# A block of Fourier filter and MLP on one core: constant tables loaded earlier, a merged first layer, and a new order of the work

## The chip, the cores and the metric

The kernel runs on one core of a Trainium2 chip. The metric is the device time of one execution in microseconds (us). Before the change three runs took 150.68, 151.34 and 151.72 us (median 151.34).

## What is computed

```
xn = layernorm(x)                                     # x: 2048 x 640, bf16
A  = irfft2( rfft2(xn) * (w_r + i*w_i) )              # over both axes
B  = gelu(xn @ w1 + b1) @ w2 + b2                     # 640 -> 1536 -> 640
out = x + A + B
```

## The kernel before

The 2048 rows are sixteen tiles of 128 rows ("tile c"). Two lines of work share the engines.

*The MLP.* DVE takes each tile's statistics (`stats`, line 479, two instructions a tile) and normalises it (`xn_c`, line 509). The result is turned into `xnT`, columns on the partitions: for tiles 0 to 5 by TensorE (`tps`, line 527) and a copy out of PSUM, for tiles 6 to 15 by a transposing DMA from SP's queue (line 518). The first layer multiplies with `W1`, which is loaded in five row blocks (`w1_0` to `w1_4`). For tiles 0 and 1 it runs in six pairs of hidden columns (`hpsa_0` to `hpsa_5`, line 573): a "pair" below is two matmuls of 128 columns, for one row block and one tile, so there are ten for each `hpsa`. For tiles 2-3, 4-7, 8-11 and 12-15 the blocks are `hps0`, `hps1`, `hps2`, `hps3`, each with twelve columns of hidden units (line 595); each is issued in two parts, row blocks 0 to 2 and then 3 and 4. ACT takes the gelu into `gT` (lines 583 and 601). The second layer sums gT with `W2`, which comes in thirds (`w2_0` to `w2_2`), in steps of four matmuls (line 751). For eight tiles (KEEP) it is done early: `kps` steps, and DVE adds the bias and keeps the sum (line 761). For the others it runs at the end (`fps`).

*The filter.* DVE folds the normalised tiles (`xe`, `xf`, lines 539 and 543), TensorE multiplies with table G (`aps`, line 549), ACT or DVE copies the result into `XV` (line 555). Then come, in six groups or four rounds, `bps` (table E, line 625), `cps` (table M, line 643), the product with the weights `W` on DVE (lines 668 and 672), and `dps` (table N, line 677), all in PSUM banks 0 to 3, each set copied out before the next may use the banks. The copies of `dps` go into buffers `U0` to `U7`, of which three exist at a time; each is turned back by two transposing DMAs (`v0` to `v15`, line 693: U0 gives v0 and v1, and so on), which wait in SP's queue. A new U may be written only when both transposes of the U that had its buffer have landed. When all v have landed, `eps` (table GE, line 716) and the last matmuls with table H (line 767) give the filter's part, which is added to the MLP's in PSUM (line 770) and stored from POOL's queue, or SP's for the last two tiles. Four DMAs from POOL's queue (`pre0` to `pre3`, line 562) write x to the output beforehand, once all of W is there.

*The order.* Nothing is scheduled at run time. Each operation has a number, and the string `ORDER` (line 253) lists all of them in one sequence; a word such as `589p:4` is operation 589 on TensorE (p; s SP, d DVE, a ACT, g POOL) with PSUM bank or buffer 4. `arrange` (line 145) gives every engine its part of the list as a strict queue, and `sync` (line 161) adds the semaphore waits that the data and the buffers need. The times in the calls of `load`, the rates, priorities and the argument `hard` serve a planner that wrote the list; the emitted program depends on the list alone. All loads of x, W1, W2, W and the tables run through SP's queue in the list's order.

Of the kernel before, what the change touches and what calls it, by code (L numbers as in the profile page):

```python
# [13 lines left out]
D = 640  # L14
F = 1536
# [238 lines left out]
9s 2a 0d 1d 3g 125p:4 11a 10s 4g 7g 8p:3 5g 12s 13s 14s 15s 54d 55d 16s 17s 56d 60d 57a 18s 58a 59d 121d:1 19s 61d 124p:2 20s 122p:1 52p:7 62d 21s 123d 126a 63d 22s 64g 241p:3  # L254
301p:4 53a 253p:0 23s 277p:5 289p:6 242p 265p:1 24s 302p 127d 290p 266p 254p 25s 278p 133d:0 128p:2 130p:7 279p 26s 129d 255p 131a 291p 243p 132d 303p 27s 267p 306p 68d 246p 294p
28s 282p 283p 66d 258p 270p 259p 69d 284p 247p 271p 292p 65d 268p 248p 249p 70d 295p 67d 307p 308p 71d 280p 136d:0 272p 72g 244p 245p 137d 250p 134d 281p 309p 251a 293p 285p 286p
141d:1 260p 252a 269p 256p 144d 296p 288a 273p 297p 135d 142p:7 287a 147d:0 145p:2 143a 298p 261p 146d 262p 274p 257p 300a 310p 148d 304p 328p:7 263a 73d 343p:2 276a 85d 337p:3
299a 329p 150d:1 84d 344p 264a 322p:6 76d 275a 319p:5 81d 345a 320p 323p 82d 330a 338p 86d 138p:0 321a 74d 139p 324a 83d 305p 75d 331p:5 87d 140a 77d 88g 334p:7 149d 332p 78d
316p:6 152d 79d 151d 335p 311a 80g 317p 173d:1 312a 346p:0 171d 347p 339a 340p:4 92d 174s 336a 341p 98d 153p:1 318a 154p 159d:0 342a 587p:6 156d 348a 172s 97d 588p 155a 163d:0
313p:4 101d 160p:0 116d 29s 589p 100d 30s 314p 93d 590p 31s 315a 162d 32s 157p:3 161a 102d 591p 94d 165d:1 99d 33s 333a 90d 592p 158a 89d 34s 325p:4 593d 326p 35s 355p:5 327a 103d  # L260
113d 36s 370p:0 91d 166d 37s 371p 167d 117d 358p:7 95d 164d 38s 96g 108d 356p 176d:0 6g 379p:6 104g 357a 118d 114d 168p:1 175d 372a 169p 184d:0 364p:5 170a 180d:1 185s 179d 365p
177d 359p 197d:1 366a 115d 380p 199d 198s 186d 373p:4 381a 178d 119d 201d:0 376p:5 120g 360a 106d 187s 182p:0 202d 377p 206d:0 181p 109d 378a 374p 200s 204d 105d 367p:6 183a 205d
110d 368p 107d 203d 39s 352p:7 188d:0 369a 40s 189d 207p:0 375a 208p 111d 41s 223d:0 112g 353p 209a 225d 406p:6 42s 190d:1 212d:1 397p:5 43s 192d 354a 191d 407p 193d 44s 210d 398p
215d:0 408a 211s 195p:0 214d 194p 399a 388p:6 219d:1 216d 196a 226s 389p 218d 217d 412p:4 227d:0 228d 221p:1 45s 220p 229d:0 385p:7 222a 213s 231d 230d 413p 232d 386p 390a 46s
234p:0 233p 414a 400p:5 47s 236d 235a 394p:6 48s 387a 457p:0,0 224s 401p 458d 459a 49s 395p 391p:4 396a 460p:0,1 361p:6 461d 462a 362p 409p:7 363a 475p:0 402a 418p:6 476d:0 477a:1
# [31 lines left out]
def bass_parallel_sum__spectral_gfnet__dense_activation_gelu__prompt_kernel(  # L297
# [21 lines left out]
    with ExitStack() as es:  # L319
# [110 lines left out]
        load_x(0, 1, next(pr), at=3.05)  # L430
        load_x(1, 1, next(pr), at=3.5)
        load(part(gT, 0, 1, 0, [[1, F]]), b1v, B_b1t, 3072, q="act", prio=409, at=3.2)
        for j, at in enumerate((5.3, 6.5, 7.7, 9.8, 10.9)):
            if j == 3:
                load_x(2, 2, next(pr), at=8.6)
            load(W1[:, F * j:F * j + F], w1v[:, j, :], B_w1s[j], 393216, prio=next(pr), at=at)
        load(gtab[:], const["G"], B_g, 524288, prio=next(pr), at=12.2)
        for c in range(4, 16, 2):
            load_x(c, 2, next(pr))
        load(b2bc[:], bass.AP(tensor=b2v.tensor, offset=b2v.offset, ap=[[0, 128], [1, D]]), B_b2b, 163840, prio=next(pr))  # L440
        for g in range(3):
            load(W2[:, 4 * g:4 * g + 4, :], w2v[:, g, :, :], B_w2s[g], 4 * D * 256, prio=next(pr))
        load(etab[:], const["E"], B_e, 204800, prio=next(pr))
        load(mtab[:], const["M"], B_m, 65536, rate=200e3, prio=next(pr))
        load(ntab[:], const["N"], B_n, 49152, rate=200e3, prio=next(pr))
        WP = 32 * KP

        def load_w(wsrc, p0, off, row, n, step):
            w_ops.append(load(bass.AP(tensor=Wf, offset=p0 * WP + off, ap=[[2 * WP, 16], [2 * KP, n], [1, 321]]),
                 bass.AP(tensor=wsrc.tensor, offset=wsrc.offset + row * 321, ap=[[128 * 321, 16], [step * 321, n], [1, 321]]),  # L450
                 B_w, 16 * 642 * n, after=[wpad], rate=145e3, issue=0.645, group="W", prio=next(pr)))
# [10 lines left out]
        load(htab[:].rearrange("p a b -> p (a b)"), const["H"], B_h, 524288, prio=next(pr))  # L462
# [103 lines left out]
        for b in range(6):  # L566
            hps = Buf(f"hpsa_{b}", psum, 1, ANY)
            pr = PRIO["hps"] + 2 - b / 10
            head = []
            for t in range(2):  # L570
                part_ = []
                for j in range(5):
                    part_ = [pe([("128", 2 * mm_us(128))], pr - j - t, lambda hps=hps, b=b, t=t, j=j: [
                        (psb(hps.slot, [[1, 128]], 256 * h + 128 * t), view(W1, F * j + 512 * (b // 2) + 2 * (b % 2) + h, [[4, 128]]), xnT[:, t, j, :], t == j == h == 0, j == 4) for h in range(2)],
                        reads=[B_w1s[j], B_xnT[t]], writes=[hps], hard=part_ + head)]
                    head = head or part_
                    l1_ops += part_
                    l1_of.setdefault(t, []).extend(part_)
            for h in range(2):
# [56 lines left out]
        for P in range(4):  # L636
# [53 lines left out]
            for pair, U, B_u in zip(two, Us, B_us):  # L690
                for qq in range(2):
                    q = 2 * pair + qq
                    K.op([("sp", 1.28)], 2000, lambda e, _, q=q, qq=qq, U=U, uv=uv: e.dma_start_transpose(  # L693
                        XV[:, :, 128 * q:128 * q + 128], uv(U, D * qq, [[1, D]])), reads=[U, B_u], writes=[B_v[q]], dma=(163840, 200e3), group=f"v{q // 2}")
# [116 lines left out]
```

## Time and profile before

| | |
|---|---|
| three runs | 150.68, 151.34, 151.72 us |
| the profiled execution's own time | 151.68 us |
| its span, first to last instruction | 149.9 us |
| busy: TensorE, weight loads, DVE, ACT, POOL | 141.9, 90.3, 111.6, 72.5, 21.9 us |
| granted TensorE clock | 1.0 throughout |
| read from and written to HBM | 13.54 MB, 5.24 MB |

The page of the profile names an instruction by engine, line, operation and out<-in; a chain at its end shows which work released which. A matmul's duration includes its run through the array, so the distance from start to start tells what a stream costs. A row of the timeline merges equal neighbours: start, length, engine, what, count, and in brackets the idle time before and what ended it. In the view of windows each engine has its busy time and, in brackets, its instructions. Some matmul records are missing (18 of the 180 first halves of the second layer's 640 columns).

### The profile page before, as it was taken

The numbers are of one execution on the slowest core, as the hardware profiler recorded it, in microseconds if no ns is written. First come the engines' busy times: TensorE is split into PE (matmuls) and PEld (weight loads), VectorE is DVE, ScalarE is ACT, GpSimd is POOL, SyncE is SP. The second block draws the span as 40 slices with busy tenths as digits, with TensorE's granted clock in tenths as the row PEclk, the third lists the DMA queues.
The fourth block names the chain that finished last, engine by engine and source line by source line (L and its number), as shares of the span: only waits on it lengthen the run. The fifth ranks groups of instructions, "written<-read, shape, count | busy, mean of one in ns | idle before, by whom it ended". The sixth has DMA issues, their size and how long they took to land.

```text
span 149.9 us, 4022 instructions
## 1 busy us (share of the span) xinstructions
PE 141.9 (95%) x1708; PEld 90.3 (60%) x1726; DVE 111.6 (74%) x238; ACT 72.5 (48%) x122; POOL 21.9 (15%) x35
## 2 busy tenths in 40 slices
PE   7999998999799999999999997999999999999993
PEld 7899985556366645446545443445676655665662
DVE  2789997999773449959877969720499889999612
ACT  3519995398577669674655734465124020031000
POOL 1101220421100040000000000000002611770420
PEclk9999999999999999999999999999999999999999
DMA  4999998996799939104600530798103392797192
GB/s 114 349 408 396 319 361 176 167 130 137 144 166 178 137 67 406 56 4 86 148 0 4 111 69 4 136 164 163 34 0 41 38 182 93 89 133 89 8 123 90
DMA packets 28499, 20.68 MB, mean 138 GB/s; under 512 B 18881, under 2 KB 25793, under 8 KB 28482
## 3 DMA queue, kind: packets, MB, share of 16 engines
q1 hardware_dynamic: 25888, 15.51, 47.7%
q0 software_dynamic: 2592, 4.92, 17.6%
q8 instruction: 13, 0.21, 0.6%
q14 instruction: 4, 0.03, 0.1%
q10 hardware_dynamic: 2, 0.00, 0.0%
HBM read 13.54 MB, written 5.24 MB: 125 GB/s over the span
## 4 chain that ended last, share of the span: by engine, by line
PE 74%; DMA 12%; SPq 6%; ACT 3%; DVE 2%; issue 2%; DVEq 0%
PE ps L383 73%; DMA W<-in_B_w_dram 9%; SPq L375 5%; DMA XV<-U 3%; ACT XV L394 2%; ACT gT L601 1%; DVE U L395 1%; DVE Xb L395 1%; DVE T L668 0%; SPq L693 0%; DVE Z L672 0%; DVE W L770 0%; PE ps L527 0%; DVEq L233 0%
## 5 line engine op out<-in xcount | busy, mean ns | idle before, releaser
L383 PE MATMUL ps<-xnT,W 128*128 128x512 bf16 (+2 forms) x360 | 58.3, 309 | 1.1 <-ACT XV L394 1.0
L383 PE MATMUL ps<-W,gT 128*128 128x128 bf16 (+3 forms) x378 | 56.6, 291 | 2.4 <-issue 1.4
L383 PEld LDWEIGHTS ps<-W,gT 128*128 128x128 bf16 x396 | 30.0, 98 | 24.2 <-issue 2.2
L383 PEld LDWEIGHTS ps<-xnT,W 128*128 128x128 bf16 x360 | 31.5, 114 | 17.9 <-ACT XV L394 1.5
L601 ACT ACTIVATE gT<-ps,b1col 128x512 bf16<-128x512 f32 (+1 forms) x48 | 28.5, 641 | 12.2 <-PE ps L383 12.0
L777 POOL DMA_DIRECT2D out_dram<-W x14 | 12.3, 1031 | 75.3 <-DVE W L770 75.3
L394 ACT ACTIVATE Wf<-ps 128x960 bf16<-128x960 f32 (+1 forms) x7 | 6.1, 893 | 24.4 <-PE ps L383 24.4
L479 DVE BATCH_NORM_STATS2 stats<-X 128x6 f32<-128x320 bf16 x32 | 14.2, 478 | 2.1 <-DMA X<-in_A_x_dram 2.1
L761 DVE TENSOR_TENSOR X<-ps,b2bc 128x640 f32<-128x640 f32 x7 | 5.8, 822 | 9.6 <-PE ps L383 9.6
L668 DVE TENSOR_TENSOR T<-Y,Wf 128x1288 bf16<-128x1288 bf16 x16 | 12.6, 823 | 0.1
L490 POOL TENSOR_TENSOR rstd<-ve,mhalf 128x2 f32<-128x2 f32 (+1 forms) x8 | 6.4, 804 | 29.8 <-DVE ve L489 29.8
L395 DVE CAST Y<-ps 128x644 bf16<-128x644 f32 x8 | 6.6, 829 | 4.3 <-PE ps L383 4.2
L394 ACT ACTIVATE XV<-ps 128x1280 bf16<-128x1280 f32 (+1 forms) x8 | 9.3, 1166 | 0.9 <-PE ps L383 0.9
L394 ACT ACTIVATE Xb<-ps 128x960 bf16<-128x960 f32 (+1 forms) x6 | 6.9, 1150 | 5.3 <-PE ps L383 5.3
L543 DVE TENSOR_TENSOR T<-T 128x512 bf16<-128x512 bf16 (+1 forms) x32 | 8.9, 312 | 0.7 <-PE ps L383 0.6
L395 DVE CAST Xb<-ps 128x960 bf16<-128x960 f32 (+1 forms) x6 | 6.8, 1134 | 3.1 <-PE ps L383 3.0
L394 ACT ACTIVATE Y<-ps 128x644 bf16<-128x644 f32 x8 | 5.6, 706 | 5.9 <-PE ps L383 5.6
L509 DVE TENSOR_SCALAR T<-X,mv,rstd 128x640 bf16<-128x640 bf16 x16 | 6.6, 440 | 1.6 <-issue 0.7
L539 DVE TENSOR_TENSOR T<-T 128x640 bf16<-128x640 bf16 x16 | 7.5, 484 | 0.2
L383 PE MATMUL ps<-getab,XV 32*128 32x160 bf16 (+1 forms) x128 | 7.6, 242 | 0.0
L383 PEld LDWEIGHTS ps<-getab,XV 32*128 32x128 bf16 (+1 forms) x128 | 6.4, 147 | 1.3 <-DVE W L770 0.2
L383 PE MATMUL ps<-etab,XV 32*128 32x160 bf16 (+1 forms) x128 | 7.2, 232 | 0.0
(51 smaller groups left out, 127.3 us busy)
## 6 DMA issues: line engine op xcount, KB each, us to landing
out_dram<-in_A_x_dram POOLq DMA_DIRECT2D x4, 640.0 KB, 6.0
X<-in_A_x_dram SPq DMA_DIRECT2D x7, 320.0 KB, 8.9
out_dram<-W POOLq DMA_DIRECT2D x14, 160.0 KB, 4.1
W<-in_B_w_dram SPq DMA_DIRECT2D x5, 384.0 KB, 5.4
W<-in_B_w_dram SPq DMA_DIRECT2D x3, 640.0 KB, 13.3
Wf<-in_A_w_r_dram SPq DMA_DIRECT2D x7, 160.5 KB, 4.1
Wf<-in_A_w_i_dram SPq DMA_DIRECT2D x7, 160.5 KB, 4.1
gtab<-c_G SPq DMA_DIRECT2D x1, 512.0 KB, 7.3
```

The lines of the kernel that those rows point to most:

```text
L375: o = K.op([(q, 1.0 if q == "pool" else issue)], prio, lambda e, _: e.dma_start(dst, src), reads=reads, writes=[buf], after=after, dma=(nb ...
L383: ins = e.matmul(o_, lhsT=lw, rhs=rh, start=st, stop=sp_, skip_group_check=True)
L394: return e.activation(dst(), src(), ACT.Copy, scale=scale)
L395: return e.tensor_copy(dst(), src())
L479: st_ops.append(K.op([("dve", 0.393)], pr, lambda e, _, c=c, h=h: e.bn_stats(stats[:, c, 6 * h:6 * h + 6], view(X, c * D + H2 * h, [[1, H2 ...
L490: K.op([("pool", 0.75)], 400 + pr, lambda e, _, a=a, b=b: e.tensor_tensor(out=rstd[:, a:b], in0=ve[:, a:b], in1=mhalf[:, a:b], op=ALU.pow) ...
L509: o = K.op([("dve", 0.356)], pr, lambda e, _, c=c, n=n, xnv=xnv: e.tensor_scalar(out=xnv(n, 0, [[1, D]]), in0=view(X, c * D, [[1, D]]), sc ...
L539: K.op([("dve", 0.39)], pr, lambda e, _, k=k, op=op, xnv=xnv, x1v=x1v: e.tensor_tensor(out=x1v(H2 * k, [[D, 2], [1, H2]]), in0=xnv(0, 0, [ ...
L543: ring_ops.append(K.op([("dve", 0.333 if w == 128 else 0.136)], pr, lambda e, _, op=op, x1v=x1v, xfv=xfv, o_=o_, o0=o0, o1=o1, w=w: e.tens ...
L601: K.op([("act", act_us(128 * nt, 1) + 0.02)], pr + PRIO["gelu"], lambda e, _, c0=c0, nt=nt, fc=fc, hps=hps: e.activation(gT[:, fc, 128 * c ...
L668: filt_ops.append(K.op([("dve", 0.738)], pr, lambda e, _, k=k, Y=Y, TB=TB, pair=pair: e.tensor_tensor(out=view(TT, TB.slot * 8 * KP + k * ...
L777: last.append(K.op([("pool", 0.9)], 450, lambda e, _, c=c, os_=os_: e.dma_start(ov[:, c, :], view(W1, OST + os_.slot * D, [[1, D]]), accum ...
```

## The change

1. The first layer of tiles 0 and 1: row blocks 3 and 4 are taken for both tiles at once, with 256 columns of `xnT[:, 0:2]`. A `hpsa` has six pairs and then two merged steps in place of ten pairs. The twelve operations fewer shift all later numbers by 12.
2. The transposes v are told to the planner to come behind the load of table H.
3. The planner's landing times and rates are replaced by others.
4. `ORDER` is new. In it, on SP: the tables e, m, n and the first two loads of W come right behind W2, ahead of the transposes of xn_7 and xn_6; the transposes of xn_8 and xn_9 come behind all loads of W but two, and behind those of tiles 10 to 13 and 15; GE and H come right behind the last load of W, ahead of all v. On TensorE: after hps0 come the kps of tiles 2 and 1 (with aps3 after them), then hps1 with kps of tiles 5 and 4, then bps. Kps 7 follows among the dps, kps 8, 10 and 11 behind hps3. On ACT: aps0 is copied ahead of the gelus of hps0. On DVE: tiles 9 to 14 get some of their statistics ahead of xn_6 and xn_7; xnT2 is copied by DVE and not by ACT; xo14 (bias plus x for tile 14) is formed early. On POOL: pre3 follows pre2 directly.

```diff
@@ loads: what the planner is told
-        for j, at in enumerate((5.3, 6.5, 7.7, 9.8, 10.9)):
+        for j, at in enumerate((6.05, 7.05, 8.02, 9.9, 10.85)):
...
-        for c in range(4, 16, 2):
-            load_x(c, 2, next(pr))
+        for c, at in zip(range(4, 16, 2), (13.55, 14.4, 15.2, 16.05, 16.85, 17.65)):
+            load_x(c, 2, next(pr), at=at)
...
-        load(htab[:].rearrange("p a b -> p (a b)"), const["H"], B_h, 524288, prio=next(pr))
+        tables = load(htab[:].rearrange("p a b -> p (a b)"), const["H"], B_h, 524288, prio=next(pr))
@@ the first layer of tiles 0 and 1
             head = []
+            done = []
             for t in range(2):
                 part_ = []
-                for j in range(5):
+                for j in range(3):
                     part_ = [pe([("128", 2 * mm_us(128))], pr - j - t, lambda hps=hps, b=b, t=t, j=j: [
-                        (... xnT[:, t, j, :], t == j == h == 0, j == 4) for h in range(2)],
+                        (... xnT[:, t, j, :], t == j == h == 0, False) for h in range(2)],
                         reads=[B_w1s[j], B_xnT[t]], writes=[hps], hard=part_ + head)]
...
+                done += part_
+            for j in range(3, 5):
+                done = [pe([("128", 2 * mm_us(256))], pr - j - 1, lambda hps=hps, b=b, j=j: [
+                    (psb(hps.slot, [[1, 256]], 256 * h), view(W1, F * j + 512 * (b // 2) + 2 * (b % 2) + h, [[4, 128]]), xnT[:, 0:2, j, :], False, j == 4) for h in range(2)],
+                    reads=[B_w1s[j], B_xnT[0], B_xnT[1]], writes=[hps], hard=done)]
...
@@ the transposes v
-                        ... writes=[B_v[q]], dma=(163840, 200e3), group=f"v{q // 2}")
+                        ... writes=[B_v[q]], dma=(163840, 200e3), group=f"v{q // 2}", hard=[tables])
```

Of the new list, the part from the last steps of hps0 to the first of hps1 (592p to 597p are kps2, 575p to 580p kps1, 153p and 154p aps1, 157p and 160p tps4 and tps5, 181p and 182p aps3, 340p hps1_1; 171d and 173d normalise tiles 6 and 7, 174s and 172s turn them):

```diff
...
+316p:0 87d 108d 88g 309a 328p:5 101d 153p:1 333a 77d 313p:4 73d 329p 314p 78d 330a 317p 75d 171d:0 592p:6 315a 79d 114d 318a 80g 593p 105d 575p:4 97d 173d 576p 156d:1 174s 577p
+176d:0 175d 594p 89d 578p 172s 99d 177d:0 154p 179d 157p:0 100d 155a 595p 34s 178d 102d 159d 579p 109d 35s 158a 596p 103d 180d 104g 110d 36s 107d 580p 162d:0 160p:3 37s 581d 597p
+161a 182p:0 111d 90d 181p 112g 340p:5 197d:0 116d 198s 6g 5g 341p 117d 358p:4 199d 342a 163d 359p 200s 113d 355p:5 164d:1 360a 91d 598d 356p 183a 38s 349p:4 165d 166d 39s 350p 115d
...
```

More of the change, by code (lines that the diff above doesn't have):

```diff
@@ L275 @@
-613g 747d 690p 622g 702p:2 757d 683p:0 654p 684d:4 691p 703d:1 692p 685g 655p 693d:2 656p 632g 740p:0 694g 731p:4 741d:0 742a 732p 657d:5 733p 744d:0 705p:0 658g 743d 745d:0 704g
-734p 746d 706a:1 707d 722p:6 723p 709d:0 724p 708d 725p 758p:1 711d:1 735p 710d 726p 736p 737p 727p 738d:0 759p 728p 739g 767p:5 719p:2 729d:2 768p 769p 770p 760p 720d:4 730g
-748p:6 749p 721g 771p 750p 772p 751p 752p 753p 754p 773p 761p 755d:1 762p 763p 764p 774d:5 776p:4 756s 777p 765d 778p 779p 780p 781p 775s 782p 766s 783d 784s
+9s 2a 1d 4g 0d 3g 8p:0 11a 10s 12s 13s 14s 15s 54d 55d 16s 17s 56d 60d 57a 18s 58a 59d 121d:1 19s 52p:1 61d 20s 124p:7 62d 122p:2 21s 63d 125p:6 126a 64g 123d 22s 53a 281p:0 241p:6
@@ new lines @@
+23s 271p:7 261p:5 7g 291p:3 127d 251p:4 24s 282p 252p 262p 133d:0 130p:1 25s 128p:2 292p 131a 272p 129d 242p 26s 293p 263p 132d 243p 254p 27s 244p 253p 245p 274p 65d 28s 264p 294p
+295p 137d:1 255p 246p 69d 29s 284p 256p 275p 68d 283p 30s 265p 247p 66d 266p 31s 273p 296p 70d 257p 67d 32s 276p 71d 248p 136d 72g 297p 134d 249a 258p 33s 285p 135d 298p 250a 267p
+141d:1 299a 277p 286p 144d 278p 260a 268p 148d:0 259a 142p:6 287p 300a 143d 145p:4 279a 288p 146d 139p:1 280a 138p 147d 270a 304p:6 84d 269a 334p:7 152d:1 325p:4 140a 81d 301p:5
@@ new lines @@
+151d 335p 82d 326p 302p 289a 149d 319p:1 303a 74d 305p 310p:3 327a 85d 320p 306a 83d 311p 76d 322p:4 336a 150d 323p 86d 312a 98d 307p:6 290a 106d 331p:7 324a 332p 92d 308p 321a
+316p:0 87d 108d 88g 309a 328p:5 101d 153p:1 333a 77d 313p:4 73d 329p 314p 78d 330a 317p 75d 171d:0 592p:6 315a 79d 114d 318a 80g 593p 105d 575p:4 97d 173d 576p 156d:1 174s 577p
+176d:0 175d 594p 89d 578p 172s 99d 177d:0 154p 179d 157p:0 100d 155a 595p 34s 178d 102d 159d 579p 109d 35s 158a 596p 103d 180d 104g 110d 36s 107d 580p 162d:0 160p:3 37s 581d 597p
@@ new lines @@
+161a 182p:0 111d 90d 181p 112g 340p:5 197d:0 116d 198s 6g 5g 341p 117d 358p:4 199d 342a 163d 359p 200s 113d 355p:5 164d:1 360a 91d 598d 356p 183a 38s 349p:4 165d 166d 39s 350p 115d
+167d 93d 352p:6 40s 351a 94d 202d:0 168p:0 41s 357a 212d:1 361p:7 201d 42s 362p 206d:0 210d 169p 363a 203d 343p:4 213s 205d 170a 344p 204d 95d 96g 353p 211s 370p:7 354a 184d:0
+208p:0 214d:0 345a 207p 215d 43s 371p 118d 219d:1 364p:4 218d 44s 372a 216d 337p:6 217d 209a 45s 735d 338p 46s 186d 365p 119d 189d:0 346p:7 120g 366a 188d 221p:0 339a 191d:0 220p
@@ new lines @@
+192d 347p 223d:1 222a 367p:6 225d 190d 226s 628p:4 193d 348a 228d:0 368p 227d 194p:1 369a 47s 195p 629p 231d:0 196a 185s 229d 611p:6 230d 232d 612p 187s 233p:1 234p 613p 236a 235d
+614p 48s 445p:0,0 224s 615p 446a 447d 616p 49s 448p:0,1 50s 617d 51s 391p:7 449a 450d 630p 392p 237g 463p:0 631p 465d:1 464a:0 238g 632p 393a 466p:0 239g 373p:7 468a 467d 240g 374p
+469d:0 427p:6 375a 474d:1 451p:0,0 470d 376p:7 452a 453d 633p 428p 473d 487p:0 429a 377p 489d:0 488a:1 382p:6 634d 383p 490p:0 472d:0 384a 388p:4 475d:1 491a 476d 389p 492d 378a
@@ new lines @@
+379p:5 390a 471d 380p 494d:0 477p:0 381a 400p:6 497d:1 479a:1 401p 478d:0 647p:4 498d 648p 480p:0 649p 481a 482d 650p 402a 745d 483s 454p:0,0 493d 485s 651p 500d:0 455a 456d 652p
+403p:6 486s 653d 404p 457p:0,1 496d:1 484s 499d 412p:5 459a 458d 394p:7 405a 495d 409p:4 504p:0 410p 506a:1 505d:0 413p 411a 395p 511p:0 396a 406p:4 513d:1 512a:0 407p 514p:0
+418p:7 516d 515a 419p 408a 517d:0 501p:0 436p:4 518d 503a 385p:6 502a 519d:1 509s 520d 386p 420a 521d:1 460p:0,0 414a 508s 522d 437p 462a 442p:7 461d 510s 387a 430p:5 523d:0 538p:0
@@ new lines @@
+524d 507s 397p:6 539d:0 540a:1 398p 438a 525p:0 433p:4 526d:2 527a:1 434p 399a 528p:0 443p 529d 530a 421p:6 435a 533s 535p:0 431p 537a 536d 422p 532s 432a 439p:4 542d:1 444a 424p:5
+541d 423a 531s 415p:1 545d:0 440p 534s 546d 664p:6 441a 425p 543d:0 665p 544d 426a 548d:1 416p 547d 683p:4 417a 666p 552p:0 667p 554d:0 553a:2 684p 549p:0 668p 551a 685p 550a 557s
+669p 686p 670d 687p 558s 688p 700p:6 689d 556s 701p 702p 555s 703p 704p 602p:4 705p 603p 706d 559p:0 566p:6 560d:1 561a 567p 563d:0 585p:0 568p 587d:0 586a 569p 570p 562d 621p:0
@@ new lines @@
+564d:1 565d 588d:0 571p 623a:1 589d 572p 604p 591d:0 622a 605p 590d 606p 573d:1 607p 624d:0 574g 608p 582p:0 609d:7 638p:6 639p 583d:5 610g 640p 625d 618p:4 641p 619d:0 657p:0
+626d:1 620g 627d 599p:4 659a:0 642p 600d:3 643p 658a 601g 674p:4 644p 661d:0 675p 645d:6 635p:0 676p 636d:2 646g 677p 654p:6 637g 693p:0 655d:7 660d 656g 710p:6 695a:1 663d:1 711p
+584g 662d 694a 678p 679p 697d:0 680p 690p:2 696d 712p 681d:0 671p:0 713p 698d:0 682g 719p:4 699d 714p 691d:3 715p 720p 672d:4 692g 716p 707p:2 673g 721p 708d:7 722p 717d:1 728p:0
@@ L278 @@
+718g 723p 730a:0 729d 724p 709g 746p:2 725p 747p 726d:5 748p 736p:6 731d:0 727g 737p 732d 755p:4 738p 733d:1 734d 749p 750p 739p 740p 756p 751p 752p 764p:5 741p 753d:4 742p 754s
+757p 758p 743d:6 759p 765p 766p 760p 767p 761p 768p 744s 769p 762d 770p 771d 763s 772s
 """
@@ L429, in bass_parallel_sum__spectral_gfnet__dense_activation_gelu__prompt_kernel @@
         pr = iter(range(999, 900, -1))
-        load_x(0, 1, next(pr), at=3.05)
+        load_x(0, 1, next(pr), at=3.02)
         load_x(1, 1, next(pr), at=3.5)
         load(part(gT, 0, 1, 0, [[1, F]]), b1v, B_b1t, 3072, q="act", prio=409, at=3.2)
-        for j, at in enumerate((5.3, 6.5, 7.7, 9.8, 10.9)):
+        for j, at in enumerate((6.05, 7.05, 8.02, 9.9, 10.85)):
             if j == 3:
-                load_x(2, 2, next(pr), at=8.6)
+                load_x(2, 2, next(pr), at=8.9)
             load(W1[:, F * j:F * j + F], w1v[:, j, :], B_w1s[j], 393216, prio=next(pr), at=at)
-        load(gtab[:], const["G"], B_g, 524288, prio=next(pr), at=12.2)
-        for c in range(4, 16, 2):
-            load_x(c, 2, next(pr))
-        load(b2bc[:], bass.AP(tensor=b2v.tensor, offset=b2v.offset, ap=[[0, 128], [1, D]]), B_b2b, 163840, prio=next(pr))
+        load(gtab[:], const["G"], B_g, 524288, prio=next(pr), at=12.15)
+        for c, at in zip(range(4, 16, 2), (13.55, 14.4, 15.2, 16.05, 16.85, 17.65)):
+            load_x(c, 2, next(pr), at=at)
+        load(b2bc[:], bass.AP(tensor=b2v.tensor, offset=b2v.offset, ap=[[0, 128], [1, D]]), B_b2b, 163840, prio=next(pr), rate=160e3, issue=0.49)
         for g in range(3):
[L442 to L445, printed above, removed]
+            load(W2[:, 4 * g:4 * g + 4, :], w2v[:, g, :, :], B_w2s[g], 4 * D * 256, prio=next(pr), rate=395e3, issue=0.49)
+        load(etab[:], const["E"], B_e, 204800, prio=next(pr), rate=340e3)
+        load(mtab[:], const["M"], B_m, 65536, rate=220e3, prio=next(pr))
+        load(ntab[:], const["N"], B_n, 49152, rate=150e3, prio=next(pr))
         WP = 32 * KP
@@ L450, in load_w @@
                  bass.AP(tensor=wsrc.tensor, offset=wsrc.offset + row * 321, ap=[[128 * 321, 16], [step * 321, n], [1, 321]]),
-                 B_w, 16 * 642 * n, after=[wpad], rate=145e3, issue=0.645, group="W", prio=next(pr)))
+                 B_w, 16 * 642 * n, after=[wpad], rate=150e3, issue=0.645, group="W", prio=next(pr)))
         for ri, wsrc in enumerate((A_w_r, A_w_i)):
@@ L569, in bass_parallel_sum__spectral_gfnet__dense_activation_gelu__prompt_kernel @@
             head = []
+            done = []
             for t in range(2):
                 part_ = []
-                for j in range(5):
+                for j in range(3):
                     part_ = [pe([("128", 2 * mm_us(128))], pr - j - t, lambda hps=hps, b=b, t=t, j=j: [
-                        (psb(hps.slot, [[1, 128]], 256 * h + 128 * t), view(W1, F * j + 512 * (b // 2) + 2 * (b % 2) + h, [[4, 128]]), xnT[:, t, j, :], t == j == h == 0, j == 4) for h in range(2)],
+                        (psb(hps.slot, [[1, 128]], 256 * h + 128 * t), view(W1, F * j + 512 * (b // 2) + 2 * (b % 2) + h, [[4, 128]]), xnT[:, t, j, :], t == j == h == 0, False) for h in range(2)],
                         reads=[B_w1s[j], B_xnT[t]], writes=[hps], hard=part_ + head)]
@@ L578, in bass_parallel_sum__spectral_gfnet__dense_activation_gelu__prompt_kernel @@
                     l1_of.setdefault(t, []).extend(part_)
+                done += part_
[3 more added lines that the diff above has]
+                    reads=[B_w1s[j], B_xnT[0], B_xnT[1]], writes=[hps], hard=done)]
+                l1_ops += done
+                for t in range(2):
+                    l1_of[t].extend(done)
             for h in range(2):
@@ L693, in bass_parallel_sum__spectral_gfnet__dense_activation_gelu__prompt_kernel @@
                     K.op([("sp", 1.28)], 2000, lambda e, _, q=q, qq=qq, U=U, uv=uv: e.dma_start_transpose(
-                        XV[:, :, 128 * q:128 * q + 128], uv(U, D * qq, [[1, D]])), reads=[U, B_u], writes=[B_v[q]], dma=(163840, 200e3), group=f"v{q // 2}")
+                        XV[:, :, 128 * q:128 * q + 128], uv(U, D * qq, [[1, D]])), reads=[U, B_u], writes=[B_v[q]], dma=(163840, 200e3), group=f"v{q // 2}", hard=[tables])
         for a, b in zip(CHAIN, CHAIN[1:]):
```

21 lines of the change are left out of this document (removed).

## The prediction, made before the changed kernel was run

> **What bounds the kernel now.** I read the page first (busy shares, clock, chain), then TensorE's waits, then the timeline at each wait, then the landings of the transfers behind them.
>
> ```profile
> span 149.9 us, 4022 instructions
> PE 141.9 (95%) x1708; PEld 90.3 (60%) x1726; DVE 111.6 (74%) x238; ACT 72.5 (48%) x122; POOL 21.9 (15%) x35
> PE 74%; DMA 12%; SPq 6%; ACT 3%; DVE 2%; issue 2%; DVEq 0%
> ```
>
> TensorE is the bound: 95% busy, and 74% of the chain. A new order can win only what TensorE waits. The view of waits names these (total, times, longest):
>
> ```profile
> PE ps L383 <- ACT XV L394: 1.0, 1, 1.0
> PE ps L383 <- DVE U L395: 0.9, 1, 0.9
> PE ps L383 <- DMA W<-in_B_w_dram: 0.5, 1, 0.5
> PEld ps L383 <- DMA W<-in_B_w_dram: 0.8, 2, 0.6
> ```
>
> The timeline gives their places (start, length, what, count, idle before); the last rows are the issue and landing of one transpose and a piece of the chain:
>
> ```profile
> 7.05 0.82 PEld L383 LDWEIGHTS ps<-xnT,W 128*128 128x128 bf16 x14 [0.22 <-DMA W<-in_B_w_dram]
> 8.14 4.63 PE L383 MATMUL ps<-xnT,W 128*128 128x128 bf16 x80
> 20.85 1.03 PE L383 MATMUL ps<-W,gT 128*128 128x128 bf16 x7
> 22.05 0.44 PE L527 MATMUL ps<-ident,T 128*128 128x128 bf16 x5
> 22.95 0.72 PE L383 MATMUL ps<-W,gT 128*128 128x512 bf16 x4 [0.46 <-DMA W<-in_B_w_dram]
> 34.51 2.32 PE L383 MATMUL ps<-xnT,W 128*128 128x512 bf16 x10
> 37.23 0.59 PE L383 MATMUL ps<-xnT,W 128*128 128x512 bf16 x2
> 38.83 1.03 PE L383 MATMUL ps<-xnT,W 128*128 128x512 bf16 x4 [1.01 <-ACT XV L394]
> 88.44 0.51 PE L383 MATMUL ps<-Z,ntab 32*32 32x320 bf16 x32
> 88.89 1.26 PE L383 MATMUL ps<-W,gT 128*128 128x512 bf16 x8
> 91.01 0.52 PE L383 MATMUL ps<-Z,ntab 32*32 32x320 bf16 x32 [0.86 <-DVE U L395]
> 90.07 0.89 DVE L395 CAST U<-ps 128x512 bf16<-128x512 f32 x2 [0.90 <-DMA XV<-U]
> ...
> 30.60 6.31 SPq L518 DMA_TRANSPOSE xnT<-T x4
> DMA to landing us min/median/max: 3.1/3.1/3.1
> ...
> 85.79 4.19 DMA XV<-U
> ```
>
> At 7.05 the weights of row block 1 of W1 land: 0.2. At 22.95 the second third of W2: five transposes from 22.05 end at 22.33 (80 matmuls of this width take 4.63, so they come 0.056 apart, the last one's drain taken off), so 0.6 is lost. At 38.83 hps2_7 starts 1.17 late (37.23 plus two steps of 0.216; ten take 2.32). The row blames ACT's copy into XV, but hps2_7 reads xnT8 to 11, and the last of the four transposes, issued at 30.60+6.31-1.28=35.63, landed 3.1 later, at 38.7: the transfer decides. At 91.01 dps2_1 waits for DVE's copy into U, which waits for v4 (issued 85.79, 4.19 to landing) to free that buffer: 0.9. Together 2.9 of 149.9.
>
> **The change, part by part.** (1) Merging. In each of six pairs of hidden columns, row blocks 3 and 4 go from eight 128-column matmuls to four of 256: 48 become 24.
>
> ```profile
> 17.24 3.00 PE L383 MATMUL ps<-xnT,W 128*128 128x128 bf16 x27
> L383 PEld LDWEIGHTS ps<-xnT,W 128*128 128x128 bf16 x360 | 31.5, 114 | 17.9 <-ACT XV L394 1.5 <-issue 1.2 <-ACT gT L601 0.5
> ```
>
> Of 128 columns they come 0.056 apart, as above; in this first row one is of 128 and 26 are of 256 columns, 0.107 each. So 48 x 0.056 - 24 x 0.107 = 0.1 is saved; the weight loads lie beside the matmuls. The merged steps wait for both tiles, but the new order mixes them with the 36 unmerged pairs, and each stands no earlier than its block's landing. By the Trainium skill, page "TensorE: Matmul & The Clock Gate", section "Back-to-back issue gap", a real stream of loads and matmuls sustains about 81 ns at 128 columns, while its formula for an isolated one of 256 gives 109; as an estimate that would make the merge worth 24 x (162-109) = 1.3 us. No row here has 81: this kernel's stream runs at the isolated gap.
>
> (2) W2.
>
> ```profile
> 103.94 2.88 PE L383 MATMUL ps<-W,gT 128*128 128x512 bf16 x20
> 106.66 1.03 PE L383 MATMUL ps<-getab,XV 128*128 128x160 bf16 x16
> ```
>
> Five steps on W2 take 103.94 to 106.66, 0.544 each. Before, TensorE meets the second third after two steps on the first. Now four steps (kps2's first two, kps1's first two) and the last two hps0 blocks (five matmuls of 0.107 each) lie ahead of it, and half of aps1 (five of 0.056) moves behind: from 20.64 (20.85 less 0.216, since one of its eight records is lost) + 2.18 + 1.07 - 0.28 = 23.6, 0.7 after the landing. The 0.6 goes; were the landing later than 23.6, each us would cost one. Next late in line is ACT.
>
> (3) The front's other engines.
>
> ```profile
> 13.95:22.90 8.95, 8.49 (x90) 7.80 (x89) 8.95 (x30) 8.40 (x19) 1.69 (x2) 1.00 1.24 337
> 18.83 0.80 DVE L509 TENSOR_SCALAR T<-X,mv,rstd 128x640 bf16<-128x640 bf16 x2
> 21.83 1.67 DVE L479 BATCH_NORM_STATS2 stats<-X 128x6 f32<-128x320 bf16 x4
> 19.65 3.14 SPq L518 DMA_TRANSPOSE xnT<-T  x2
> DMA to landing us min/median/max: 4.2/4.9/5.5
> ```
>
> In that window (PE, PEld, DVE, ACT busy) DVE has nothing idle and ACT 0.55. The new order puts eight more statistics (0.40 each) and the copy of xnT2 ahead of xn_6 and xn_7, so these move from 19.6 to about 23.3; xn_5 ends 11 instructions later and xf3 another 3, at 0.30 each (30 in 8.95) 26.6 and 27.5. On TensorE, from 23.6 on, seven W2 steps, half of aps1 and tps4 lie ahead of tps5 (28.0), one step more ahead of aps3 (28.8), and hps1 stands at 29.4: covered by 1.4 and 1.3. ACT now copies aps0 before most gelus of hps0; at its share a hole of some tenths moves there: 0 to 1.0 (TensorE's longest wait laid to ACT in the view of waits); I take 0.4, nearest to ACT's 0.55 of idle time, which is all the room it has to catch up.
>
> (4) SP's queue.
>
> ```profile
> 9.06 1.42 SPq L375 DMA_DIRECT2D W<-in_B_w_dram  x3
> ```
>
> e, m, n and two loads of W pass xnT7 and xnT6. They issue in SP's idle time from 10.5 on (9.06+1.42; SP then waited until 19.65), and their bytes queue behind W2. xnT7 and xnT6, issued from 23.3 on, take 3.14 to issue and landed 4.2 to 5.5 after issue with that much in front: the second, issued at 24.9, lands between 29.1 and 30.4 at worst, and at 27.5 with the 2.6 of an empty queue. hps1 needs it at 29.4: 0 to 1.0, I take 0.1, since their 0.5 MB is then gone. xnT8 and xnT9 move behind all but two loads of W and five other transposes, the last xnT15; xn_15 comes 47 DVE instructions after xf3, near 43 with its three long additions, so xnT9 issues near 46.4 and lands between 49.0 and 51.9 (2.6 to 5.5 later). Ahead of hps2 TensorE has, from 29.4, twelve hps1 blocks (1.08), five aps (0.56), eight W2 steps and two bps (about 2.2): 51.9. The 1.17 goes. Were xnT9 later, hps2 would wait for the difference, with nothing else in that place.
>
> (5) The way back.
>
> ```profile
> 71.78 0.58 SPq L375 DMA_DIRECT2D getab<-c_GE  x1
> 94.99 0.58 SPq L375 DMA_DIRECT2D htab<-c_H  x1
> DMA to landing us min/median/max: 5.2/5.5/5.9
> 98.07 0.51 PE L383 MATMUL ps<-Z,ntab 32*32 32x320 bf16 x32
> 99.48 1.20 SPq L693 DMA_TRANSPOSE XV<-U  x1
> 103.38 1.28 SPq L693 DMA_TRANSPOSE XV<-gtab  x1
> DMA to landing us min/median/max: 2.6/2.7/3.2
> ```
>
> getab and htab took SP 0.58 each among V's transposes, and htab's bytes held v10 and v11 to 5.2 to 5.9 instead of 2.6 to 3.2. Now both go right behind the last load of W, some 18 us ahead of V's first transpose by SP's count, with nothing due. TensorE never waited for v10 or v11 (last landing 106.0, eps0 at 106.66), so by itself this buys no time, only 0.6 for v0 to v3. The three places where PE hangs on V: a dps ends 0.45 after its start (88.44 to 88.89), the first transpose issues 0.96 later (98.52 to 99.48), each next 1.30, and lands 2.65 after issue; the third lands 6.2 and the fourth 7.5 after that end. dps1_1 (U2's buffer needs v1, fourth): 8.3 of PE work in between, spare 0.8. U5 after dps2_0 (needs v7, now third; v4, fourth, before): 6.6, spare 0.4. eps0 (needs the fourth): 14 steps of 0.544 (five take 103.94 to 106.66) = 7.6, spare 0.1. So the 0.9 goes, with thin cover: I take 0.3 for the three (0 to 3.1, below).
>
> (6) Banks. Both copies of dps1_0 on ACT (as before), bps0 right behind aps7, and the final blocks, where four banks turn over behind DVE: 0 to 1.0, I take 0.4. pre3 moves up to its three siblings on POOL, right behind W, and its bytes leave V's time. The tail (last matmul, copy, store) keeps its form: 0.
>
> Of the wait for W1's block 1 half is filled, since six matmul pairs and not five stand ahead of it.
>
> Sum: gone 0.1 + 0.6 + 1.2 + 0.9 + 0.1 (merge) = 2.9; new 0.4 + 0.1 + 0.3 + 0.4 = 1.2; net -1.7. The profiled execution took 151.68, span 149.9; it would be 150.0, span 148.2. The median of the runs, 151.34, lies 0.34 lower: 149.6.
>
> **The rivals.** A: waits move, not go. DVE and ACT are full in the front and banks turn over just in time, so all upper ends of (3), (4) and (6) apply (3.0 for 0.9): 149.6 + 2.1 = 151.7 at most, 150.7 in the middle. For it: 8.95 of 8.95 in the front; against it: over the span DVE is 74% and ACT 48% busy.
>
> B, slower: late transposes. v4 took 4.19 instead of 2.65 with no table in front of it; why, no row says.
>
> ```profile
> DMA to landing us min/median/max: 2.6/2.7/4.2
> ```
>
> If the transpose that counts is late by x at all three places, PE waits (x-0.8)+(x-0.4)+(x-0.1). At x = 1.55 that is 3.3, less my 0.3: 152.6. It ends above 151.34 once x passes about 1.1. Against it: only one of the four in that row was late, and of the last four none took over 3.2.
>
> C, full gain: all covers hold: 148.4.
>
> D: weight loads set the pace of the 128-column stream. The load row gives 31.5/360 = 0.0875 each, so 24 x (0.175-0.107) = 1.6 more: 148.0. Against it: 80 in 4.63. The Trainium skill's 81 ns would come to nearly the same.
>
> **How the numbers follow.** Forecast 149.6 (149.1 to 150.2) 0.45, A 0.27, C 0.14, D 0.03, B 0.11. The range goes from D's 148.0 to A's upper end, 151.7; outside it lie B and what I overlooked, not 2 in 10. One per cent (1.5 us: 149.8 and 152.9) is about what a measurement of this kernel can tell from no change. Faster by more: two thirds of the forecast, C, D: 0.47. Slower by more: a third of B and what I overlooked: 0.08. Within: 0.45.
>
> **What would show it.** Right: no wait for W2; hps1 near 29.4, hps2 near 51.8, eps0 near 108 without a gap over 0.3; no wait for U; htab landed before 60; last matmul near 145.3. Wrong: a gap ahead of hps1 or hps2 of over 0.5, a new wait for V at eps0, a front later than 29.9, or bank waits over 1 in the final blocks. If the span falls by 1.5 with the waits still there, the merge did it (D).

## The result and the profile after

Six runs of the changed kernel have a median of 149.16 us, six of the kernel before 151.69: a ratio of the means of 0.9844 (95% interval 0.9811 to 0.9876), 1.6% faster. A later set on another occasion gave 148.98 against 151.70 (0.9825, 0.9795 to 0.9856). The profiled execution took 148.61.

The page of after, its span, busy shares and chain:

```profile
span 146.8 us, 3994 instructions
...
PE 142.9 (97%) x1702; PEld 89.9 (61%) x1702; DVE 111.7 (76%) x241; ACT 72.8 (50%) x119; POOL 21.2 (14%) x35
...
PE 94%; DVE 3%; DMA 2%; issue 0%
```

All that TensorE still waits for in after, as far as the view of waits names it (the first is the start of the kernel, the second stands at 6.32):

```profile
PE ps L383 <- DVE warm L399: 1.0, 1, 1.0
PE ps L383 <- DVE xnT L395: 0.2, 1, 0.2
```

The timeline of after at five places, where before waited or where the prediction feared a new wait: the steps on W2, the first of hps1, the first of hps2, dps2_1, and eps0. No row has idle time before it:

```profile
21.21 3.10 PE L383 MATMUL ps<-W,gT 128*128 128x512 bf16 x21
...
29.13 1.67 PE L383 MATMUL ps<-xnT,W 128*128 128x512 bf16 x7
...
51.44 0.84 PE L383 MATMUL ps<-xnT,W 128*128 128x512 bf16 x3
...
89.19 0.52 PE L383 MATMUL ps<-Z,ntab 32*32 32x320 bf16 x32
...
107.47 1.03 PE L383 MATMUL ps<-getab,XV 128*128 128x160 bf16 x16
```

So the waits went that make up 2.8 of the sum's 2.9, and of the 1.2 that should have come in their place almost nothing came. That leaves the question what removed them: the order, the merge, or the tables.

### The profile page after: what moved, and what is told of

It reads as the page before. It is cut to its first block, busy times and chain, and to the rows that moved or that the text cites. A ratio compares the mean times of both kernels' runs of the same rounds, so it can differ in the third digit from the quotient of the medians.

```text
span 146.8 us, 3994 instructions
## 1 busy us (share of the span) xinstructions
PE 142.9 (97%) x1702; PEld 89.9 (61%) x1702; DVE 111.7 (76%) x241; ACT 72.8 (50%) x119; POOL 21.2 (14%) x35
## 4 chain that ended last, share of the span: by engine, by line
PE 94%; DVE 3%; DMA 2%; issue 0%
PE ps L383 93%; DMA X<-in_A_x_dram 2%; DVE stats L479 1%; PE ps L527 1%; DVE W L779 0%; DVE T L509 0%; DVE mv L481 0%; DVE xnT L395 0%; DVE rstd L487 0%; DVE ve L489 0%
## 5 line engine op out<-in xcount | busy, mean ns | idle before, releaser
L383 PE MATMUL ps<-W,gT 128*128 128x512 bf16 (+3 forms) x396 | 58.1, 295 | 0.0
L394 ACT ACTIVATE Wf<-ps 128x960 bf16<-128x960 f32 (+1 forms) x9 | 7.9, 909 | 27.1 <-PE ps L383 27.1
L490 POOL TENSOR_TENSOR rstd<-ve,mhalf 128x2 f32<-128x2 f32 (+1 forms) x8 | 5.8, 719 | 34.3 <-DVE ve L489 34.3
L543 DVE TENSOR_TENSOR T<-T 128x128 bf16<-128x128 bf16 (+1 forms) x32 | 8.9, 312 | 0.7 <-PE ps L383 0.6
L733 DVE TENSOR_TENSOR Wf<-Wf 128x960 bf16<-128x960 bf16 (+1 forms) x12 | 6.9, 597 | 1.2 <-ACT Wf L394 1.1
```

The costliest lines, as they stand in the source:

```text
L383: ins = e.matmul(o_, lhsT=lw, rhs=rh, start=st, stop=sp_, skip_group_check=True)
L394: return e.activation(dst(), src(), ACT.Copy, scale=scale)
L490: K.op([("pool", 0.75)], 400 + pr, lambda e, _, a=a, b=b: e.tensor_tensor(out=rstd[:, a:b], in0=ve[:, a:b], in1=mhalf[:, a:b], op=ALU.pow) ...
L543: ring_ops.append(K.op([("dve", 0.333 if w == 128 else 0.136)], pr, lambda e, _, op=op, x1v=x1v, xfv=xfv, o_=o_, o0=o0, o1=o1, w=w: e.tens ...
L733: K.op([("dve", 0.068 + n / 6)], pr + 2, lambda e, _, k=k, op=op, yo=yo, y2=y2, n=n: e.tensor_tensor(out=view(Wf, Y2 + y2.slot * 3 * D + ( ...
```

## The experiments

Twelve runs. Medians below stand beside those of the kernel before on the same chip: 151.57 for the first four, 151.46 for the next four, 151.70 for the last four. In after and its variants the lines behind 573 are numbered up to 9 higher (L702 there is L693 here).

**First four: one part at a time.** `e_moves` takes before's list and moves only this:

```diff
-589p 314p ... 157p:3        +314p 157p:3 589p
-406p:6 ... 361p:6 362p      +361p:6 362p 406p:5   (banks 4 to 7 renamed behind it)
-540p:0 641p ... 642p        +641p 642p 540p:0
```

> The list of before, with nothing but TensorE's work moved at the three places where it waited (and the gelu that belongs to a moved block): the second half of hps0_0 and tps4 go ahead of the first step on w2_1; hps1_4 goes ahead of hps2_7; two steps of kps5 go ahead of dps2_1. No merge, GE and H stay among the v, SP's queue is untouched. Theory 1 (the gain of the change is work put into these three waits): 0.5 of the 0.62 at 22.95, 1.1 of the 1.17 at 38.83 and 0.8 of the 0.86 at 91.01 go, so 2.4 us less than before: 149.2. Rival (the merge brings 1.5 of the gain): the moves alone bring 1.0, 150.6. Rival A (waits move on to other engines): 0.8 less, 150.8, with new waits of 1.6 behind DVE or ACT.

Measured: 151.1, ratio 0.9971 (0.9945 to 0.9997). Neither theory: barely faster. The three waits are gone from the view, but others stand in their place; the view of waits, and the largest of them in the timeline:

```profile
PE ps L383 <- ACT Xb L394: 0.6, 1, 0.6
PE ps L383 <- ACT gT L601: 0.2, 1, 0.2
```
```profile
52.25 0.50 PE L383 MATMUL ps<-Xb,mtab 32*32 32x322 bf16 x32 [0.63 <-ACT Xb L394]
```

At the last block ahead of cps0_0 (52.07 in before) TensorE was 1.29 ahead of before, at cps0_0 itself 0.56: hps1_4, pulled forward by 12 us, no longer covers the copy there. This profile also started 0.7 later than that of before (tps0 at 5.98 and 5.27). This hand-made order did what rival A foretold. Filling the waits does not bring their length by itself.

`e_tables` is before with `50s 51s` (GE and H) right behind `49s`.

> The list of before, with GE and H alone moved: both right behind the last load of W. Theory 1: nothing, 151.6 (within 0.3 of before), and the wait for U at 91 stays, since v4 is late for another cause: a block of 16 KB of TensorE's instructions, read at 87.8 while v4 is under way, and the tables do not move that block. Rival (the tables in the way of v make the wait for U): 0.9 less, 150.7, v4 lands 2.65 after its issue.

Measured: 151.68, ratio 0.9991 (0.9961 to 1.0021): nothing. v4, with no table near it, is late again (V's transposes from 81 to 92 us):

```profile
  DVE U L395: 1.1, 1
...
DMA to landing us min/median/max: 2.6/2.6/4.4
```

`e_merge` is before with the merge alone (the code of after, before's list, each merged step in the place of the later of its two).

> The list of before, with the merge alone: row blocks 3 and 4 of W1 for tiles 0 and 1 at once. Theory 1: the merge itself brings 0.1, and TensorE's first steps of hps0 start within 0.2 of where they stood. But TensorE has 48 instructions fewer ahead of 87.8, so the block of instructions read there should be read 48 instructions later, near 88.6, when v4 (due at 88.4) has landed: then the 0.86 at 91.01 goes too, 150.7 in all. If the block has nothing to do with v4, the wait for U stays, 151.5. Rival D (weight loads pace the 128-column stream): 1.3 to 1.6 less at 6 to 14 us, 150.2 or below, whatever becomes of v4.

Measured: 149.62, ratio 0.9874 (0.9839 to 0.9909): three quarters of the whole gain, from a part that I had priced at 0.1. It is not rival D. Set against before matmul by matmul, the profiled TensorE is 0.80 behind at the first of hpsa (a late start, see below), 0.75 behind at the first hps0 block and 0.85 once the last merged step is through: no gain there. (On the way before lost 0.23 to block 1 of W1, e_merge 0.31 ahead of a tps at 12.96.) It is 0.13 behind just ahead of hps2_7, 1.04 ahead at it and 1.81 ahead from dps2_1 on. Both waits went, though nothing was moved at either. The timeline of ACT and of TensorE there also settles who held hps2_7 in before: its stream runs through 37.8 without a gap, while ACT's copy into XV still lasts until 38.8.

```profile
37.56 1.24 ACT L394 ACTIVATE XV<-ps 128x1280 bf16<-128x1280 f32 x1
```
```profile
37.36 1.89 PE L383 MATMUL ps<-xnT,W 128*128 128x512 bf16 x8
```

`e_split` is the reverse: after's order with each merged step split in two again.

> The kernel after with the merge alone taken back (row blocks 3 and 4 of W1 once for each of the tiles 0 and 1 again, in the places of the merged steps). Theory 1: 0.1 more than after. But 48 instructions of TensorE more move the block of instructions that after reads at 108.3 to about 106.3, 1.6 behind the issue of v12, the last transpose that eps0 needs: v12 lands 1.0 to 1.8 later, eps0 waits as long, and the time is 150.3 to 151.0 with the loss at 107 us. If the block has nothing to do with the landings: 149.3. Rival D: 150.5 to 150.8 as well, but lost between 6 and 14 us, with eps0 not waiting.

Measured: 150.1, ratio 0.9887 (0.9853 to 0.9921), about 1 above after. The profiled TensorE is 0.5 behind after from 7.8 us on (block 1 of W1 landed late), 0.6 once hpsa is through, and 1.6 behind from eps0 on, which waits for a late transpose of V. The timeline, V's last four transposes, and the DMA queues from 102.5 to 107.7 (packets, MB, share):

```profile
109.07 1.07 PE L383 MATMUL ps<-getab,XV 128*128 128x160 bf16 x16 [0.90 <-DMA XV<-U]
```
```profile
DMA to landing us min/median/max: 2.6/3.2/4.5
```
```profile
q1 hardware_dynamic: 2038, 0.50, 75.5%
q8 instruction: 1, 0.02, 1.4%
```

The q8 row is one packet of 16 KB, a block of TensorE's instructions. It was read at 104.7 (I had expected 106.3), 2.1 after v15's issue; v15 landed after 4.5, and v13 and v12 behind it came late as well. In after the same view from 100.8 to 107.4 has no such row.

**Next four: the blocks.** `e_fetch` has the list and the work of before. Only the dummy matmuls ahead of the first input change:

```diff
-    39 matmuls of 128 columns on zeros
+    8 matmuls of 512 columns and 7 of 128 on zeros
```

> The list and the whole work of before; only the first group of dummy matmuls that TensorE runs ahead of the first input is changed: eight of 512 columns and seven of 128 in place of 39 of 128. The columns are the same, the instructions 48 fewer. Theory B (blocks of 16 KB of TensorE's instructions, read while transposes are under way, made the waits at 38.83 and 91.01; the merge gained by shifting them): the blocks read at 32.3 and 87.8 come some 48 instructions later, as in the kernel with the merge alone, xnT11 lands near 37.1 and v4 in time, both waits go, 1.9 less than before: 149.7. Rival (the merge itself, or the order, brings the gain; the blocks are harmless): 151.6, with both waits in place.

Measured: 149.54, ratio 0.9884 (0.985 to 0.9917). The view of waits has no transfer, no XV and no U left:

```profile
PE ps L383 <- issue: 1.4, 9, 0.2
PE ps L383 <- DVE warm L399: 1.0, 1, 1.0
```

(The nine of `issue`, 0.16 each, stand in before's view as well.) Set against before matmul by matmul, the profiled e_fetch is 0.16 ahead just before hps2_7, 1.34 from there on, and 2.26 from dps2_1 on: the two waits, 1.18 and 0.92, are its gain. Its own late start, 0.8 at the first of hpsa, was gone at the step on w2_1, where before waits.

How the blocks did it is seen at the four transposes xnT8 to xnT11. Before, with the DMA queues from 30.6 to 38.8 (packets, MB, share):

```profile
L518 SPq DMA_TRANSPOSE xnT<-T x4: 1221/1280/2397, 30.6 to 35.6; - x4
...
DMA to landing us min/median/max: 2.6/3.7/4.9
```
```profile
q1 hardware_dynamic: 3209, 0.97, 95.3%
q8 instruction: 1, 0.02, 1.2%
q14 instruction: 1, 0.01, 0.3%
```

and e_fetch, with the queues from 30.4 to 36.9, where the last has landed:

```profile
L518 SPq DMA_TRANSPOSE xnT<-T x4: 1223/1278/1283, 30.4 to 34.3; - x4
...
DMA to landing us min/median/max: 2.5/3.1/4.2
```
```profile
q1 hardware_dynamic: 3246, 0.99, 101.7%
```

With the block (at 32.3) one issue took 2.40 instead of 1.28 and the last transpose landed at 38.7; without it, at 36.8. The longer issue is 1.1 of these 1.9, enough to bring the landing to 37.6, where hps2_7 was due (37.66). Most of the rest is the last transpose itself, 3.1 from issue to landing and not 2.5; there another engine's block (q14, 8 KB, at 37.5) was read in before and not in e_fetch. Whether that block cost this 0.6, no run separates.

The same at v4, issued at 85.79, with the 4.19 that no row explained to me. The DMA queues of before from 85.79 to 90:

```profile
q1 hardware_dynamic: 1322, 0.32, 39.1%
q8 instruction: 1, 0.02, 1.4%
```

V's transposes from 81 to 92 in e_fetch:

```profile
DMA to landing us min/median/max: 2.6/2.6/2.7
```

By the Trainium skill, page "Runtime: NRT & Kernel Launch", section "Instruction fetch mechanics", an engine's instructions come in blocks of 16 KiB, 256 instructions, over a DMA queue of its own, and crossing a block is "mostly hidden". The size agrees with the page's row (13 packets, 0.21 MB). The views name no wait of TensorE for a block of its own; for a transpose in flight the cost was 1.5 to 2.0 us (4.2 to 4.6 from issue to landing, and not 2.6 to 2.7).

`e_split_fetch` gives e_split the shorter group of dummies.

> The new order with the merge taken back, as in the run before, and the same shorter group of dummy matmuls: 48 instructions more and 48 fewer. Theory B: the blocks stand where they stand in after, v12 and v13 land in time, the wait of 0.9 at eps0 goes, 149.3 (0.1 above after for the merge). Rival D (the merge itself is worth 0.9 or more): 150.1, as without the shorter group.

Measured: 149.36, ratio 0.9863 (0.9832 to 0.9894). The blocks are back where after has them, and eps0 starts without a wait. Against after's 149.16 and 148.98 the merge by itself is worth 0.2 to 0.4 between medians, with intervals that overlap. Rival D's 1.3 to 1.6 falls a second time.

```profile
108.17 1.02 PE L383 MATMUL ps<-getab,XV 128*128 128x160 bf16 x16
```

`e_tables_late` is after with `50s` behind `486s` and `51s` behind `532s`; `e_warm` is after with `125p` right behind `8p` and `52p` behind `122p`.

> The kernel after with GE and H put back among the v: GE behind the third of the first four, H behind the second of the third four, as they stood in before. Theory 1: v1 comes 0.6 later, v8 and v11 some 3 later, and the covers hold but for up to 0.5 behind dps1_1, where v1 is already the last of four: 149.2 to 149.7. Rival (the early tables are what the change lives on): 150.1 or more, with a wait for U or at eps0.

> The kernel after with the first matmuls in the order of before: all 47 dummy matmuls, then tps0, then the transposing of b1. After has 39, b1, tps0 and the last 8 behind tps0. The dummy matmuls come 0.085 apart until some moment between 3.5 and beyond 5.5, and 0.056 apart from then on; that moment differs from execution to execution. Theory: where it is late, the 47 end near 5.9 and tps0 starts at 6.0 and not at 5.2, so the median rises by 0.3 to 0.7, 149.5 to 149.9. Rival (the start is taken up by a later wait, as the wait for W2 took it up in before): 149.2.

Measured: e_tables_late 149.95 (0.9891, 0.9854 to 0.9927), e_warm 148.91 (0.9838, 0.9809 to 0.9867). The order of the first matmuls is worth nothing, though in this profiled execution the pace changed early and tps0 started at 5.35. The dummies come 0.107 apart until the change, not 0.085 as I wrote. The loss of e_tables_late was larger than expected and stood, in its profile, mostly ahead of 8.2, so it ran again.

**Last four.** `e_after` is after itself; `e_tables_late2` is e_tables_late; `e_short` has `WARM = (32, 4)` for `(39, 8)`; `e_emn` has `29s` to `33s` behind `172s`.

> The kernel after once more, as the yardstick of the three others on the same chip: 149.2 (149.0 to 149.4). The first two stretches differ from execution to execution (when the dummy matmuls fall from 0.107 to 0.056 apart; when block 1 of W1 lands), so its spans should spread by about 1 us.

> The kernel after with GE and H among the v again, a second time. In the first profile the tables cost 0.13, all at cps2_0 behind dps1_1; the rest of its loss stood ahead of 7.1, where nothing was changed. Theory (the tables are worth 0.1 in this order): 0.1 to 0.2 more than after on the same chip, 149.3. Rival (they are worth the 0.8 by which the first medians differ): 149.9 again, with a loss behind 70 us of over 0.4.

> The kernel after with fewer dummy matmuls: 32 and 4 in place of 39 and 8. Where they stay 0.107 apart to the end, the 39 and b1 last until 5.8, while xn_0 is there at 5.2; with 32 they end near 5.05, and hpsa starts near 6.3 and not at 7.1. Where the pace changes early, nothing is gained. Theory: the start is on the path in after, so the median falls by 0.2 to 0.5, to 148.8, and the spread narrows. Rival (fewer dummies make the pace change later, and the first real matmuls pay): 149.2 to 149.5. 22 instructions fewer move the blocks of instructions by less than 1 us, and none onto the last of four transposes.

> The kernel after with the tables e, m, n and the first two loads of W put back behind the transposes of xn_7 and xn_6. My prediction put 0.1 (0 to 1.0) on having them in front. Theory: xnT7 and xnT6 land up to 0.5 earlier with nothing in front, hps1 does not wait for them either way, W and the tables come some 2 later, and all of W still lands ahead of its first use at 55: 149.2, within 0.2 of after. Rival: the loads of W that then follow push xnT10 and xnT11 and the later transposes by 2 us, hps2 waits: 150 or more.

Measured: e_after 148.98 (148.68 to 149.12, a spread of 0.4 and not 1). e_tables_late2 149.52 (0.9863, 0.9831 to 0.9895): 0.5 above after, of which its profile shows 0.16 at cps2_0, behind v1, and 0.30 ahead of 6.7. e_short 149.48 (0.9863, 0.9815 to 0.9911): no gain, since hpsa started at 6.4 but then waited 0.38 for block 1 of W1. It also lost 0.4 at cps2_0. Against what I had expected, a block (at 75.2) did fall onto the last of four transposes there, v1, issued at 73.5 and landed after 4.2; DVE's copy waited for it, and TensorE for the copy:

```profile
78.74 0.50 PE L383 MATMUL ps<-Xb,mtab 32*32 32x322 bf16 x32 [0.33 <-DVE gtab L395]
```

e_emn 149.61 (0.9881, 0.9841 to 0.992): 0.6 above after, of which its profile shows 0.12 at aps4 (44.67 in e_after) and 0.46 ahead of 7.4. So the early tables are worth something between the 0.1 or 0.2 that their places show and the 0.5 of the medians. Why the starts of these kernels should differ, with the same code there, stays open.

## Why the prediction was right, and where it was not

**Right.** 149.6 was forecast, 149.16 measured. Every wait of before that it named went, and the blocks stood near the forecast places: hps1 at 29.13 (forecast 29.4), hps2 at 51.44 (51.8; the terms given for 51.9 add up to 51.7), eps0 at 107.47 (108). H landed at 56.4 (forecast: ahead of 60), and TensorE's last matmul began at 144.04 (145.3).

**(1) Merging, 0.1: right as a price, wrong as a whole.** From the first matmul of hpsa to aps0 the profiled e_split_fetch loses 0.06 to after (0.63 behind, then 0.69) and nothing behind that, so most of the 0.2 to 0.4 between the medians is its later start. (Matmuls of 256 columns start 0.109 apart and not 0.107, as the prediction read them; its sum then gives 0.05.) But the merge takes 48 instructions out of TensorE's stream, and I costed only their time. Put alone on the kernel before it brought 1.9, because the blocks of code behind it were read at other moments.

**(4) and (5), the causes.** "The transfer decides" at 38.83 was right, e_merge shows it against ACT's copy. That the transfer was late because of a block of code, and v4 too, I did not see; of v4 I wrote that no row says why. The page's q8 row and the DMA queues of those 4 us do. So "the 1.17 goes" and "the 0.9 goes" came true, yet in before both go with the order untouched (e_fetch). The new order's own worth depends on where the blocks lie: where they lie badly, 151.57 to 150.1 (before, e_split); where they lie well, 149.54 to 149.36 (e_fetch, e_split_fetch), which a measurement hardly tells from nothing. So part of the forecast time was reached by luck: nothing in the prediction placed the blocks, and with the same order and 48 instructions more (e_split) eps0 waits 0.9. That the tables buy no time was right in before's order.

**(2) W2.** The wait at 22.95 is gone in after, as forecast. In e_merge it is gone too, with a start 0.8 later: the step on w2_1 stands at 23.18, behind the landing (21.93 there, 22.91 in before). So it takes up a late start and is worth 0.6 only after an early one. With the wait gone a late start stays: e_after starts hpsa 0.38 later than after's first profile and its last matmul 0.40 later.

**(3) to (6), the new waits: mis-sized.** 0.4 + 0.1 + 0.3 + 0.4 were taken, 0.1 at most came (0.08 of it ahead of dps2_0). The covers held, the thin one behind dps1_1 against rival B itself: after has a block at 73.7, two of V's transposes there are late, and DVE's copy waits 1.1 for v1 (the buffer's name in the row is that of its memory). The view of V's transposes from 68 to 78, and TensorE at the same place:

```profile
  DVE gtab L395: 1.1, 1
...
DMA to landing us min/median/max: 2.6/3.2/4.4
```
```profile
75.78 0.52 PE L383 MATMUL ps<-Z,ntab 32*32 32x320 bf16 x32
76.22 1.49 PE L383 MATMUL ps<-xnT,W 128*128 128x512 bf16 x6
77.64 0.50 PE L383 MATMUL ps<-Xb,mtab 32*32 32x322 bf16 x32
```

TensorE has no gap at 77.64. Rival B's mechanism exists: e_split shows it at eps0, where the cover was 0.1, for 0.90, and e_short at cps2_0, behind dps1_1, for 0.4. That after escapes it at both is where its blocks happen to lie. With the new waits at zero the sum is 151.68 - 2.9 = 148.8, and the profiled execution, the fastest of its six, took 148.61: it went as rival C had it, and the median lies between C and the forecast.

## What to carry to other kernels

Where one transfer of a kind lands late for no visible reason, look for an instruction row in the DMA queues of that window before believing in the order around it. A change in the number of an engine's instructions moves every later block of its code; to price the change itself, hold that number fixed with dummy instructions, as e_split_fetch does. A wait for a landing that does not depend on when the engine started hides a late start, so its removal brings its full length only after an early one.

## What the runs showed of the hardware that I had not expected

In these traces V's transposes landed 2.6 to 2.7 after issue wherever no block, no table and no late transpose was in their way. In the fifteen cases where a block of TensorE started 1.7 to 2.25 us after an issue and no table was near, that transpose took 4.2 to 4.6, and one issued right behind it 3.3 to 3.7. In after the blocks at 81.7 and 90.2 started 0.6 and 0.4 ahead of an issue, and those transposes took 2.6.

The start of TensorE varies from execution to execution of the same kernel. The dummies of after, in the first profile and in e_after's:

```profile
1.03 3.59 PE L383 MATMUL ps<-warm 128*128 128x128 bf16 x39 [1.03 <-DVE warm L399]
4.55 0.55 PE L383 MATMUL ps<-ident,gT 1*128 1x1 bf16 x12
```
```profile
1.03 4.34 PE L383 MATMUL ps<-warm 128*128 128x128 bf16 x39 [1.03 <-DVE warm L399]
5.30 0.56 PE L383 MATMUL ps<-ident,gT 1*128 1x1 bf16 x12
```

From the first dummy to the row behind them it is 3.52 in the one and 4.27 in the other. In e_after their starts lie 0.107 apart to the end, in after only until 3.7 and 0.056 from there, while the granted clock reads 1.0 in both. The Trainium skill, page "TensorE: Matmul & The Clock Gate", Part 1, has such a change of pace, from 106.7 to 55.6 ns at 128 columns, around 4 us into sustained work, give or take 0.5. Both paces agree (0.107 and 0.056). The moment spreads wider here: without a pause in the stream, at 3.7 in after and at 6.2 in e_merge, that is 2.7 and 5.2 us after the first matmul.
